# Another order for a planned kernel: nudged priorities, small halves last, recalibrated plan costs

## The chip, the cores and the metric

The kernel runs on one core of a Trainium2 chip. The metric is the device time of one execution in microseconds; the median over several runs counts. Five engines work side by side, each through its own instructions in the order in which they were written: TensorE (PE in the profile; its weight loads are PEld), VectorE (DVE), ScalarE (ACT), GpSimd (POOL) and SyncE (SP), which here only issues DMAs.

## The reference

Three stages follow each other. A delta rule runs over 768 positions for 32 (batch, head) pairs with a 48 x 48 state; a gated MLP (384 to 2048 to 384) works on the resulting 3072 tokens; a mixture of eight experts (384 to 1024 to 384) follows, weighted by a Sinkhorn-normalised gate:

```python
for t in range(S):                          # attention, S = 768
    y[:, :, t] = einsum('bhd,bhde->bhe', q_t, state)
    v_old = einsum('bhde,bhd->bhe', state, k_t)      # k_t normalised
    state = state + beta_t * einsum('bhd,bhe->bhde', k_t, v_t - v_old)
h = x @ w_in; x = (h * sigmoid(h)) @ w_out           # first MLP
P = exp(x @ w_gate - max)
for _ in range(8):                          # Sinkhorn
    P /= P.sum(1) + 1e-9; P /= P.sum(0) + 1e-9; P *= N / E
for e in range(E):
    out += P[:, e:e+1] * (maximum(x @ w1[e], 0) @ w2[e])
```

All is in float32, with inputs laid out by the host in their memory order only.

## The kernel before

**Halves.** Every large product is done in three matmuls of a rounded type: an operand is split into a high half (rounded by ACT) and a low half (what is left, by DVE or POOL); high x high, high x low and low x high are added up in PSUM.

**Attention and first MLP, interleaved.** Attention goes in 12 steps s of 64 positions. For a pair j of steps, `tri(j)` inverts small triangular matrices on DVE, 31 times a product (L555) and a subtraction (L553), then a scaling (L568). ACT copies the result (L571), SP writes it to DRAM (`rd`, `td`) and reads it back transposed (`rt`, `td`; L595, L603). Then each step is a chain of narrow matmul groups on PE with copies by ACT and DVE between: `z` (L614), `r` (L627), `c` (L646), `d` (L665), `y` (L680), the state's update `s` (L696, added by DVE in L701) and the transpose `t` (L713). The next step starts from that state. `gkq` (L405, L406) are the grams of keys and queries of later steps, whose loads `ke` go through SP.

Two steps make a batch b of 512 tokens for the first MLP, six batches in all. Each has 16 groups f: `moe_h` (PE, `h`, nine 128x512 matmuls, L740), the sigmoid on ACT (L746), the product on DVE (`sg`, L750), the high half on ACT (L754), the low half on POOL (`g`, L758), and `moe_o` (PE, `x2p`, nine matmuls, L782). The weights of this MLP are split in the kernel too, in 20 pieces, most of two groups f: `weight` loads one (`wr`, L869), ACT takes its absolute value and its high half (L873, L891) and DVE does seven instructions (L894, L895, L897, L899, L901, L903 and L905, which writes the low half in `w`). They are used six times; the first batch is where they must come in time.

**Experts.** Then the Sinkhorn normalisation (small PE groups `sk`, DVE and POOL) and 64 rounds of the expert stage. A round has 15 products `p` (L1213, three 128x512 matmuls each), whose results DVE, ACT and POOL add up and split, and 12 outputs `o` (L1300, six 128x384 matmuls each).

**What sets the order.** Nobody writes the order by hand: class `Order` is a list scheduler. Each group of work is added with its engine, a planned cost, its dependences and a priority (`add`). `emit` steps through a model of the run: for each engine it collects what could start (`ready`), takes among those within NEAR of the earliest the one with the highest priority (on PE, one of the same `turn` as the two before it is put back by ALT), advances the engine by the planned cost, and writes the instructions in that order. The plan's times are nothing but numbers in that model; on the chip an instruction waits for what it really needs. Until the first `moe_h`, `emit` also fills PE's planned gaps with matmuls on constant data (`idle`).

## Time and profile before

| | |
|---|---|
| runs of the kernel before (3) | 2260.31 us median, 2255.88 to 2264.96 |
| the profiled execution | 2263.14 us, span 2261.4 us |
| mean granted TensorE clock | 0.974 |
| busy PE / PEld | 2184.4 us (97%) / 1928.4 us (85%) |
| busy DVE / ACT / POOL | 1760.9 us (78%) / 1023.8 us (45%) / 1547.7 us (68%) |
| the chain that ended last, by engine | PE 64%, POOL 13%, DVE 10%, DMA 5%, issue 4%, ACT 2% |

The span is counted from the first to the last instruction; the rows below count their times from its start. The profile cuts the span into stretches with the busy time of each engine, so a stage can be read by itself: PE is idle for 77 us of the whole, and the granted clock says how much of the rest ran at the lower of the two levels (0.5 is 1.2 GHz, 1.0 is 2.4 GHz). Idle time on an engine that is not the last to be waited for costs nothing.

### The profile page before, as it was taken

The numbers are of one execution on the slowest core, as the hardware profiler recorded it, in microseconds if no ns is written. First come the engines' busy times: TensorE is split into PE (matmuls) and PEld (weight loads), VectorE is DVE, ScalarE is ACT, GpSimd is POOL, SyncE is SP. The second block draws the span as 40 slices with busy tenths as digits, with TensorE's granted clock in tenths as the row PEclk, the third lists the DMA queues.
The fourth block names the chain that finished last, engine by engine and source line by source line (L and its number), as shares of the span: only waits on it lengthen the run. The fifth ranks groups of instructions, "written<-read, shape, count | busy, mean of one in ns | idle before, by whom it ended". The sixth has DMA issues, their size and how long they took to land.

```text
span 2261.4 us, 40411 instructions
## 1 busy us (share of the span) xinstructions
PE 2184.4 (97%) x15750; PEld 1928.4 (85%) x15750; DVE 1760.9 (78%) x2999; ACT 1023.8 (45%) x1766; POOL 1547.7 (68%) x1387
## 2 busy tenths in 40 slices
PE   8988799999999899999999999989999999999999
PEld 8877578788877778889998999979999999999998
DVE  7695857464725698888888888897888888888887
ACT  2443333334344445454444545455454444445453
POOL 0223344445337688888788888877888888888884
PEclk9887999998989899999999999999999999999999
DMA  9767132314140201101111111111101111111101
GB/s 266 186 201 167 56 72 66 81 52 95 40 108 11 84 29 31 40 29 36 35 36 36 33 38 29 43 47 39 42 29 36 36 36 36 36 36 30 42 29 50
DMA packets 127424, 136.79 MB, mean 60 GB/s; under 512 B 83392, under 2 KB 91328, under 8 KB 127232
## 3 DMA queue, kind: packets, MB, share of 16 engines
q1 hardware_dynamic: 124864, 133.55, 21.4%
q8 instruction: 124, 2.03, 0.4%
q10 hardware_dynamic: 2368, 0.66, 0.2%
q14 instruction: 68, 0.56, 0.1%
HBM read 108.47 MB, written 25.69 MB: 59 GB/s over the span
## 4 chain that ended last, share of the span: by engine, by line
PE 64%; POOL 13%; DVE 10%; DMA 5%; issue 4%; ACT 2%; SPq 1%; DVEq 0%; POOLq 0%; ACTq 0%
PE o L1300 25%; PE p L1213 20%; PE x2p L782 6%; PE h L740 5%; DVE s L1022 4%; POOL room L1022 3%; POOL wa L1022 3%; POOL wraw L1022 2%; POOL h L1022 2%; DMA ke<-in_kq 2%; PE d L665 1%; POOL wb L1022 1%; DMA nd<-ke 1%; DVE acc L1316 1%; PE y L680 1%
## 5 line engine op out<-in xcount | busy, mean ns | idle before, releaser
L1213 PE MATMUL p<-room,wa 128*128 128x512 f32 x2880 | 732.8, 395 | 2.6 <-DVE s L1022 2.6
L1213 PEld LDWEIGHTS p<-room,wa 128*128 128x128 f32 x2880 | 537.2, 189 | 95.6 <-issue 3.0
L1300 PE MATMUL o<-wb,room 128*128 128x384 f32 x2784 | 601.2, 337 | 10.6 <-POOL room L1022 3.0
L1022 DVE TENSOR_TENSOR s<-s,p 128x512 f32<-128x512 f32 x704 | 475.8, 683 | 167.8 <-ACT s L1227 85.1
L1300 PEld LDWEIGHTS o<-wb,room 128*128 128x128 f32 x2784 | 496.7, 188 | 34.8 <-DVE acc L1316 9.3
L1022 POOL TENSOR_TENSOR room<-s,room 128x512 fp32r<-128x512 f32 x232 | 321.0, 1384 | 222.0 <-ACT s L1246 117.0
L1316 DVE SCALAR_TENSOR_TENSOR acc<-o,pr,acc 128x384 f32<-128x384 f32 x708 | 415.7, 610 | 15.0 <-PE o L1300 12.6
L1300 PE MATMUL o<-wb,h 128*128 128x384 f32 x1824 | 416.5, 336 | 6.1 <-DVE acc L1316 3.7
L1300 PEld LDWEIGHTS o<-wb,h 128*128 128x128 f32 x1824 | 327.7, 188 | 27.7 <-DVE acc L1316 2.8
L1022 POOL TENSOR_TENSOR wa<-wraw,wa 128x640 fp32r<-128x640 f32 x189 | 322.4, 1718 | 2.5 <-ACT wa L1116 2.5
L1244 ACT ACTIVATE room<-s 128x512 fp32r<-128x512 f32 x232 | 145.7, 628 | 382.5 <-DVE s L1022 382.3
L1022 POOL TENSOR_TENSOR wraw<-wraw 128x256 f32<-128x256 f32 x378 | 275.0, 748 | 20.5 <-issue 10.7
L758 POOL TENSOR_TENSOR g<-sg,g 128x512 fp32r<-128x512 f32 x96 | 129.8, 1353 | 219.9 <-ACT g L754 206.0
L1246 ACT ACTIVATE s<-s 128x512 f32<-128x512 f32 x384 | 243.1, 633 | 12.2
L782 PE MATMUL x2p<-g,w 128*128 128x512 f32 x864 | 228.9, 412 | 15.5 <-DVE w L905 5.8
L1116 ACT ACTIVATE wa<-wraw 128x640 fp32r<-128x640 f32 x189 | 138.2, 731 | 224.4 <-POOL wraw L1022 213.6
L1022 DVE TENSOR_TENSOR s<-p,s 128x512 f32<-128x512 f32 x320 | 219.5, 686 | 16.7 <-PE p L1213 2.0
L740 PE MATMUL h<-x,w 128*128 128x512 f32 x864 | 216.9, 398 | 5.9 <-DVE w L905 4.1
L782 PEld LDWEIGHTS x2p<-g,w 128*128 128x128 f32 x864 | 165.1, 196 | 59.3 <-POOL g L758 10.7
L1022 POOL TENSOR_TENSOR h<-s,h 128x512 fp32r<-128x512 f32 x152 | 208.7, 1373 | 7.9 <-ACT s L1246 7.8
L1022 DVE TENSOR_TENSOR s<-s,s 128x512 f32<-128x512 f32 x192 | 207.3, 1080 | 2.5
L740 PEld LDWEIGHTS h<-x,w 128*128 128x128 f32 x864 | 161.6, 190 | 44.2 <-DVE w L905 5.9
(177 smaller groups left out, 2260.9 us busy)
## 6 DMA issues: line engine op xcount, KB each, us to landing
wraw<-in_w SPq DMA_DIRECT2D x126, 384.0 KB, 3.0
kv<-in_kv SPq DMA_DIRECT2D x12, 768.0 KB, 5.8
ke<-in_kq SPq DMA_DIRECT2D x40, 192.0 KB, 4.4
kqp<-in_kq SPq DMA_DIRECT2D x40, 192.0 KB, 4.0
nd<-ke SPq DMA_DIRECT2D x20, 256.0 KB, 4.1
gd<-ke SPq DMA_DIRECT2D x20, 256.0 KB, 2.8
kqp<-gd SPq DMA_DIRECT2D x40, 128.0 KB, 3.8
wr<-in_w_in SPq DMA_DIRECT2D x6, 768.0 KB, 5.8
```

The lines of the kernel that those rows point to most:

```text
L665: nc.tensor.matmul(out=ps[o:o + 64, h], lhsT=rt[o:o + 64, bp, h], rhs=w[o:o + 64, h], start=True, stop=True)
L680: nc.tensor.matmul(out=ps[0:64, h], lhsT=t(slice(0, 112), 1)[:, h], rhs=x[0:112, 0, h], start=True, stop=True)
L740: nc.tensor.matmul(out=ps.rearrange("p (s t) -> p s t", s=2), lhsT=w[:, k, wl], rhs=X1[:, at, k, xl], start=n == 0, stop=n == 8)
L758: nc.gpsimd.tensor_tensor(out=g[:, 1], in0=T["sg", b, f], in1=f32(g)[:, 0], op=ALU.subtract)
L782: nc.tensor.matmul(out=T["x2p", b][j], lhsT=w[:, wl, 128 * j:128 * j + 128], rhs=g[:, gl], start=f == 0 and n == 0, stop=f == NF - 1 and n ...
L1022: e.tensor_tensor(out=out, in0=in0, in1=in1, op=o)
L1116: nc.scalar.activation(P2[key][:, :, 0], R(3 + 5 * g, 8 + 5 * g), AF.Copy)
L1213: nc.tensor.matmul(out=ps, lhsT=w[:, i, wl], rhs=x[:, xl], start=k == 0, stop=k == 2)
L1244: nc.scalar.activation(P2[key][:, 0], buf(x), AF.Relu)
L1246: op2("ACT", 0.52, lambda: nc.scalar.activation(buf(x), buf(x), AF.Relu), writes=[("s", n, x)], prio=PR_H)
L1300: nc.tensor.matmul(out=ps, lhsT=h[:, hl, 128 * i:128 * i + 128], rhs=w[:, wl], start=c == 0, stop=c == 5)
L1316: op2("DVE", 0.53, lambda A=A, pk=pk, t=t: nc.vector.scalar_tensor_tensor(out=A(), in0=P2[pk], scalar=P2["pr"][:, t, e:e + 1], in1=A(), op ...
```

## The change

Nothing is computed otherwise, and every engine has as many instructions as before, but for the `idle` matmuls: 347 instead of 283. What changes is the order.

- A table NUDGE of some 120 entries adds a number to the priority of a kind of operation (its engine, the function that issues it, its old priority). ALT and the NEAR windows get other values.
- Planned costs, the landing times of DMAs, latencies between instructions of one engine and the numbers of the plan's model of TensorE's clock are replaced by others. DVE additions with two inputs in SBUF and POOL's sums and low halves are now planned as excluding each other (`port`).
- In the plan alone, the reader of a split operand may start before its low half is done: by 1.2 us for `moe_o` (LATE), 0.45 (activations) or 0.85 (weights) for `moe_h` (SOON), 0.59 for the outputs (REST). The instructions still wait for the data.
- To go with that, the nine matmuls of a group are written with the half as the outer loop: those that read the second operand's low half, or the weights', come last.
- Where two engines' candidates start at the same planned time, the one that is ready earlier goes first.

```diff
-ALT = 9.5
+ALT = 12.4
-NEAR_DVE = 0.29
+LATE, SOON, REST = -1.2, -0.45, -0.59
+NEAR_DVE = 0.0
+NUDGE = {
+    ('DVE', 'weight', 1.5): -5.0, ('DVE', 'tri', 4): -3.8, ('PE', 'merge.z', 10): -4.9,
...
     def add(self, engine, cost, fn, ...
+        prio += NUDGE.get((engine, name, round(prio, 2)), 0.0)
...
-                if best is None or t < best[0]:
-                    best = (t, i, e)
+                if best is None or (t, r) < best[:2]:
+                    best = (t, r, i, e)
...
-            for k in range(KD):
-                for wl, xl in ((0, 0), (0, 1), (1, 0)):
+            for wl, xl in ((0, 0), (0, 1), (1, 0)):
+                for k in range(KD):
...
-        O["g", b, f] = [h, l]
+        O["g", b, f] = [h, (l, LATE)]
...
-            for j in range(KD):
-                for n, (wl, gl) in enumerate(((0, 0), (1, 0), (0, 1))):
+            for n, (wl, gl) in enumerate(((0, 0), (1, 0), (0, 1))):
+                for j in range(KD):
```

On DVE, before, the last turns of the first triangular inverse (`tri(0)`: `tmpu` and `tu` are its product and its result) stood alone:

```order
L555 TENSOR_TENSOR tmpu_97<-nu_95,tu_96 128x87
L553 TENSOR_TENSOR tu_96<-tu_96,tmpu_97 128x3x29
L555 TENSOR_TENSOR tmpu_97<-nu_95,tu_96 128x60
L553 TENSOR_TENSOR tu_96<-tu_96,tmpu_97 128x2x30
L555 TENSOR_TENSOR tmpu_97<-nu_95,tu_96 128x31
L553 TENSOR_TENSOR tu_96<-tu_96,tmpu_97 128x31
L568 TENSOR_TENSOR tu_96<-tu_96,du_100 128x1024
```

Now weight pieces (`w4`, `wt8`, `wt10`, `wr2`) stand between them; the changed kernel's L605, L607 and L620 are the L553, L555 and L568 of before, its L945 to L956 the weights' L894 to L905:

```order
L607 TENSOR_TENSOR tmpu_97<-nu_95,tu_96 128x87
L956 SCALAR_TENSOR_TENSOR w4_699<-wr1_525 128x2x384
L605 TENSOR_TENSOR tu_96<-tu_96,tmpu_97 128x3x29
L945 TENSOR_SCALAR wt8_771<-wt8_771 128x768
L607 TENSOR_TENSOR tmpu_97<-nu_95,tu_96 128x60
L946 TENSOR_SCALAR wt8_771<-wt8_771 128x768
L605 TENSOR_TENSOR tu_96<-tu_96,tmpu_97 128x2x30
L948 SCALAR_TENSOR_TENSOR wt8_771<-wr2_639,wt8_771 128x768
L607 TENSOR_TENSOR tmpu_97<-nu_95,tu_96 128x31
L945 TENSOR_SCALAR wt10_804<-wt10_804 128x768
L605 TENSOR_TENSOR tu_96<-tu_96,tmpu_97 128x31
L620 TENSOR_TENSOR tu_96<-tu_96,du_100 128x1024
```

In all, 19 weight instructions moved into the tail of this inverse: two pieces whole and five instructions of the next.

On DVE, in the first batch, the conversion of piece `wt20` (weights of groups 8 and up) stood behind the state updates of step 3 (`xs0_91<-xs0_91,s3_0`) and the masked keys of later steps (`kqp`):

```order
L447 TENSOR_TENSOR kqp1_86<-kqp1_86,mask_101 64x512 x2
L555 TENSOR_TENSOR tmpu_97<-nu_95,tu_96 128x31
L510 TENSOR_REDUCE ne4_2938<-sq4_0_2939 128x8
L701 TENSOR_TENSOR xs0_91<-xs0_91,s3_0_2941 48x384 x2
L510 TENSOR_REDUCE ne4_2938<-sq4_1_2961 128x8
L447 TENSOR_TENSOR kqp2_87<-kqp2_87,mask_101 64x512 x2
L894 TENSOR_SCALAR wt20_2343<-wt20_2343 128x768
L895 TENSOR_SCALAR wt20_2343<-wt20_2343 128x768
```

Now `w20` is complete within the second triangular inverse, ahead of the product `sg0_6` of the first batch:

```order
L605 TENSOR_TENSOR tu_96<-tu_96,tmpu_97 128x20x12
L950 TENSOR_SCALAR wr5_1882<-wr5_1882 128x768
L607 TENSOR_TENSOR tmpu_97<-nu_95,tu_96 128x247
L952 SCALAR_TENSOR_TENSOR wr5_1882<-wr5_1882 128x768
L605 TENSOR_TENSOR tu_96<-tu_96,tmpu_97 128x19x13
L954 TENSOR_SCALAR wr5_1882<-wt22_2062 128x768
L956 SCALAR_TENSOR_TENSOR w20_2228<-wr5_1882 128x2x384
L801 TENSOR_TENSOR sg0_6_2395<-h0_6_2361,sg0_6_2395 128x512
```

All 20 pieces now stand ahead of the last product of the first batch (`sg0_15`). Between `sg0_0` and the end of the second triangular inverse, DVE has 55 weight instructions, 62 of the inverse and 10 products (25, 52 and 6 before).

On PE, before, the first group of step 2 (`z2`) stood ahead of `h0_8`:

```order
L614 MATMUL z2_2453<-rt_93,td11_94 32x32 x32
L740 MATMUL h0_8_2490<-x1_106,w16_2424 128x512 x9
L627 MATMUL r2_2515<-zt2_2501,td11_94 32x32 x32
L740 MATMUL h0_9_2555<-x1_106,w16_2424 128x512 x9
L665 MATMUL d2_0_2577<-wq2_0_1712,rt_93 64x48 x16
L665 MATMUL d2_1_2602<-wq2_1_1752,rt_93 64x48 x16
```

Now it stands behind the `x2p` group of f = 11 (here the last three of its matmuls), so that 12 of the batch's 16 groups lie ahead of it:

```order
L833 MATMUL x2p0_0_1973<-g0_11_2835,w20_2228 128x512
L833 MATMUL x2p0_1_1974<-g0_11_2835,w20_2228 128x512
L833 MATMUL x2p0_2_1975<-g0_11_2835,w20_2228 128x512
L665 MATMUL z2_2890<-rt_93,td11_94 32x32 x32
L833 MATMUL x2p0_0_1973<-g0_12_2879,w24_2483 128x512
L833 MATMUL x2p0_1_1974<-g0_12_2879,w24_2483 128x512
L833 MATMUL x2p0_2_1975<-g0_12_2879,w24_2483 128x512
```

Between the last `x2p` of a batch and the first `h` of the next, some 17 narrow groups followed each other at the ends of the fourth and the fifth batch; now about 7 and 4 do. The Sinkhorn groups `sk` start later and stand further apart. In the rounds of the expert stage behind them, PE's order of products and outputs is the same.

## Rows read from the trace of the kernel before

**Rows 1.** Stretches of the span: length, then busy time of each engine.
```profile
core 0: us, PE busy (x) PEld busy (x) DVE busy (x) ACT busy (x) POOL busy (x), PEclk, DMA share, GB/s
0.00:106.00 106.00, 95.04 (x1799) 89.78 (x1799) 71.66 (x229) 37.74 (x68) 17.99 (x27) 0.89 0.88 231
106.00:263.00 157.00, 134.54 (x1860) 109.80 (x1856) 125.39 (x243) 67.12 (x111) 47.74 (x42) 0.87 0.57 151
263.00:743.00 480.00, 461.69 (x4568) 377.90 (x4567) 262.14 (x485) 177.63 (x322) 234.93 (x222) 0.96 0.27 64
743.00:860.00 117.00, 106.54 (x505) 91.80 (x504) 98.22 (x180) 61.09 (x110) 91.99 (x93) 0.94 0.17 58
860.00:1500.00 640.00, 636.99 (x3223) 576.60 (x3221) 553.56 (x860) 313.05 (x534) 541.96 (x472) 1.00 0.11 34
```

**Rows 2.** Timeline of PE, batches 0 and 1: start, length, engine, line.
```profile
106.12 1.21 PE L740 MATMUL h<-x,w 128*128 128x512 f32 x4
262.46 1.43 PE L740 MATMUL h<-x,w 128*128 128x512 f32 x5
```

**Rows 3.** Timeline of PE in the middle of a later batch.
```profile
586.83 2.20 PE L740 MATMUL h<-x,w 128*128 128x512 f32 x9
588.87 2.20 PE L782 MATMUL x2p<-g,w 128*128 128x512 f32 x9
```

**Rows 4.** What PE waited for, 106 to 263 us: total, times, longest.
```profile
PE gkq L405 <- DMA ke<-in_kq: 9.0, 4, 4.4
PE x2p L782 <- DVE w L905: 4.4, 2, 3.1
PE h L740 <- DVE w L905: 4.1, 3, 1.7
```

**Rows 5.** Timeline of DVE: end of the first inverse, then step 3 and `wt20`.
```profile
48.43 1.23 DVE L568 TENSOR_TENSOR tu<-tu,du 128x1024 f32<-128x1024 f32 x1
...
207.22 1.12 DVE L701 TENSOR_TENSOR xs<-xs,s 48x384 f32<-48x384 f32 x2 [2.04 <-PE s L697]
...
212.57 1.09 DVE L894 TENSOR_SCALAR wt<-wt 128x768 f32<-128x768 f32 x1
```

**Rows 6.** The chain that ended last, from 55 to 60 us, and at 175 us.
```profile
55.23 3.62 DMA ke<-in_kq
58.88 1.12 SPq L576
...
174.92 1.13 PE z L614 x64
```

**Rows 7.** Groups by line, DVE, 106 to 263 us: busy, mean ns, idle.
```profile
L553 DVE TENSOR_TENSOR tu<-tu,tmpu 128x112 f32<-128x112 f32 (+15 forms) x43 | 17.5, 408 | 0.9
...
L897 DVE SCALAR_TENSOR_TENSOR wt<-wr,wt 128x768 int32<-128x768 int32 (+1 forms) x15 | 12.6, 840 | 0.2
...
L899 DVE TENSOR_SCALAR wr<-wr 128x768 int32<-128x768 int32 (+1 forms) x15 | 8.0, 532 | 0.0
```

**Rows 8.** Timeline of ACT: the copy behind the second inverse.
```profile
158.52 2.09 ACT L571 ACTIVATE nu<-tu 128x1024 f32<-128x1024 f32 x1
```

**Rows 9.** Three shorter stretches; columns as in rows 1.
```profile
554.00:568.00 14.00, 14.00 (x186) 13.27 (x185) 5.90 (x15) 4.32 (x11) 9.04 (x11) 0.51 0.34 112
656.00:667.00 11.00, 11.00 (x168) 10.74 (x163) 2.94 (x7) 4.14 (x10) 2.09 (x3) 0.53 0.12 39
200.00:300.00 100.00, 82.00 (x710) 65.39 (x709) 81.16 (x174) 35.92 (x65) 31.29 (x30) 0.88 0.28 78
```

**Rows 10.** What PE waited for, 263 to 743 us; columns as in rows 4.
```profile
PE x2p L782 <- POOL g L758: 5.1, 6, 1.3
```

**Rows 11.** Timeline of POOL and DVE around 228 us.
```profile
228.32 1.46 POOL L758 TENSOR_TENSOR g<-sg,g 128x512 fp32r<-128x512 f32 x1 [0.80 <-ACT g L754]
228.54 1.64 DVE L897 SCALAR_TENSOR_TENSOR wt<-wr,wt 128x384 int32<-128x384 int32 x1
...
233.03 0.56 DVE L897 SCALAR_TENSOR_TENSOR wt<-wr,wt 128x384 int32<-128x384 int32 x1
```

More of the change, by code (lines that the diff above doesn't have):

```diff
@@ L60 @@
     QUEUES = ("SP",)
+    OWN = {"PE": 0.0, "DVE": 0.12, "ACT": 0.12, "POOL": 0.11, "SP": 0.08}
     LAT = {"PE": 0.2, "ACT": 0.16, "DVE": 0.14, "POOL": 0.1, "SP": 0.08}
@@ L67, in __init__, with add @@
         self.pools, self.slot = {k: [()] * n for k, n in pools.items()}, {}
-    TICK, PHASE, FULL = 10.24 / 3, 2.63, 2000
-    def add(self, engine, cost, fn, deps=(), prio=1.5, take=(), turn=None, cols=768, port=False):
+    TICK, PHASE, FULL, KEEP = 10.24 / 3, 2.53, 1000, 120
+    def add(self, engine, cost, fn, deps=(), prio=1.5, take=(), turn=None, cols=0, port=False, lands=None):
+        name = fn.__qualname__.replace("kernel.<locals>.", "").replace(".<locals>", "").replace(".<lambda>", "")
+        prio += NUDGE.get((engine, name, round(prio, 2)), 0.0)
         d = [x if isinstance(x, tuple) else (x, None) for x in deps]
-        self.ops.append((engine, cost, fn, d, prio, take, turn, cols, port))
+        self.ops.append((engine, cost, fn, d, prio, take, turn, cols, port, lands))
         return len(self.ops) - 1
@@ L99, in ready @@
             if lat is None:
-                lat = 0.0 if own == engine and engine not in self.QUEUES else self.LAT[own]
+                lat = self.LAT["SP"] if self.ops[d][9] else (self.OWN if own == engine else self.LAT)[own]
             at = max(at, end[d] + lat)
@@ L150, in emit @@
                         lane = lanes[-8] + 0.1 if e in self.QUEUES and len(lanes) >= 8 else 0.0
-                        c.append((max(r, now[e], lane, port["POOL" if e == "DVE" else "DVE"] if self.ops[i][8] else 0.0), i))
+                        r = max(r, now[e])
+                        c.append((max(r, lane, port["POOL" if e == "DVE" else "DVE"] if self.ops[i][8] else 0.0), i, r))
                 if not c:
@@ L185, in emit @@
                         order.append((now[e], len(order), None))
-                        now[e] = self.pe(now[e], 0.107, 256)
+                        now[e] = self.pe(now[e], 0.107, 80)
                     t = max(t, now[e])
-                    narrow = turn == 1 and cols != 150
+                    narrow = cols in (520, 221, 240, 390, 480, 530)
                     if narrow != tiled:
@@ L632, in merge @@
         sc.free(a, "a", [e1, e2])
-        c = O["r1", s] = op("PE", 1.13, r, [e1, e2] + O["tdl", s], prio=7.5 + FIRST[s], take=["a"], turn=1 if s else None, cols=512)
+        c = O["r1", s] = op("PE", 1.13, r, [e1, e2] + O["tdl", s], prio=7.5 + FIRST[s], take=["a"], turn=1 if s else None, cols=221)
         sc.free(a, "sg", [c])
@@ L785, in moe_o @@
         a = O["o", b, f] = op("PE", 2.045, pe, O["g", b, f] + O["wout", f] + prev, prio=4.5,
-                              take=["x"] if f == 0 else [], turn=0, cols=4608)
+                              take=["x"] if f == 0 else [], turn=0, cols=1430)
         sc.free(O["g", b, f][0], "g", [a])
@@ L996, with op2 @@
     last, lastw, readers, touched = NSTEP - 1, {}, {}, {}
-    def op2(engine, cost, fn, reads=(), writes=(), deps=(), **kw):
+    def op2(engine, cost, fn, reads=(), writes=(), deps=(), late=(), **kw):
         own = {"DVE": 0.13, "ACT": 0.14, "POOL": 0.1}
@@ L1003, in op2 @@
             x = lastw[k]
-            d.append((x, own.get(engine)) if sc.ops[x][0] == engine else x)
+            d.append((x, own.get(engine)) if sc.ops[x][0] == engine else (x, REST) if k in late else x)
         for k in writes:
@@ L1234, in add @@
             i = op2("DVE", 0.6, lambda: tt("DVE", buf(x), get(a), get(b), o), reads=[key(y) for y in (a, b) if y != x],
-                    writes=[("s", n, x)], take=["s"] if new else [], prio=PR_A)
+                    writes=[("s", n, x)], take=["s"] if new else [], prio=PR_A,
+                    port=PORT and isinstance(a, str) and isinstance(b, str))
             if new:
@@ L1302, in outputs @@
                 a = P2["pe"] = op2("PE", 1.042, pe, reads=[("h", n, f, j) for f in range(2)] + [("wb", wn(n), f) for f in range(2)], writes=[pk],
-                        deps=[(P2["pe"], 0.0)], take=["m"], turn=3, cols=2304, prio=PR_O)
+                        deps=[(P2["pe"], 0.0)], late=[("h", n, f, j) for f in range(2)], take=["m"], turn=3, cols=716, prio=PR_O)
                 if first and m == 0:
```

153 lines of the change are left out of this document (91 added, 62 removed), and 14 rows, old and new, of the table NUDGE.

## Prediction, made before the changed kernel ran

> **What bounds the kernel now.** I first read the busy time by stretches, cut where the stages change [rows 1]. From 860 us on, PE is busy 636.99 of 640 us at a granted clock of 1.00: the reader is to see an engine with nothing to give there but its own work. The other stretches are different. Ahead of the first `h` (0 to 106 us) no wide work exists. In the first batch (106 to 263, the starts of `h0_0` and `h1_0` [rows 2]) PE is busy 134.54 of 157 us at clock 0.87. In the batches behind it the idle time is 480 - 461.69 = 18.3 us at 0.96, around the Sinkhorn stage 117 - 106.54 = 10.5 us at 0.94. So about 11 + 22.5 + 18.3 + 10.5 = 62 us of PE's idle time, and nearly all its time at the lower clock, lie before 860 us.
>
> Second, a later batch in its steady state: `h` at 586.83 and `x2p` at 588.87, 2.04 us a group [rows 3]. Two groups alternate at that pace and nothing waits. The floor of the first batch is then, with 32 such groups, 65 us and the narrow groups. From rows 1: a mean clock of 0.87 means that 26% of 157 us = 41 us went by at 1.2 GHz; work done there would take half as long at 2.4 GHz, so at least 134.54 - 20 = 114 us stay.
>
> Third, why the first batch takes 157 us: the waits [rows 4] name the grams' loads (9.0 us) and the weights' low halves (4.4 + 4.1). The second lot is an order of DVE: step 3's state update stands at 207.22 (with a wait for PE before it), and piece `wt20` begins only at 212.57 [rows 5], so PE waits behind it for the weights of groups 8 and up. DVE had time, and stood behind narrow PE work.
>
> **The change, part by part.** The sum is made on the profiled execution, 2263.1 us, of which 2261.4 are the span; the median shown is 2.8 us lower.
>
> (1) *Start, +9.* 19 weight instructions now lie in the tail of the first inverse. Seven kinds take from 840 (L897) to 532 ns (L899) [rows 7], in the middle 0.69, so 13.0 us later ends L568, which ended at 49.66 [rows 5]. On the chain, the second write of `rd` (L576) went out at 58.88 behind a load that landed at 58.85 [rows 6], not behind the inverse: with the copy's 2.09 [rows 8] it could have gone at 51.8. Up to 7 us of the 13 are therefore cover, if the loads keep their place; but SP now also issues two more weight loads and two key loads ahead of it, and PE has five more gram groups to do before `h0_0`. Bounds 0 (the weights would otherwise have been done later, but still ahead of `h0_0`, and cost DVE there) and +13; I take +9, nearer to the inverse's price, since the rest of that chain is serial.
>
> (2) *First batch, 157 to 135: -22.* All pieces stand ahead of `sg0_15`, so the 8.5 us of waits for weights [rows 4] go, and the loads `ke`, of which two more go early, wait less. What is late next is the second inverse: step 2 needs it. Count DVE from `sg0_0` to its end: before 25 weight instructions, 52 of the inverse, 6 products; at 0.69, 0.41 (408 ns, L553 [rows 7]) and 0.69, as the products are of the same width, 42.7 us. In the trace the copy behind it starts 158.52 - 106.12 = 52.4 us after the first `h` [rows 2, 8], so 9.7 us are start-up and waits. Now 55, 62 and 10 make 70.3; with the same 9.7 the copy starts at +80. From the copy to `z2` it was 174.92 - 158.52 = 16.4 us [rows 6, 8]: +96. From `z2` to the end of step 3's update 208.34 - 174.92 = 33.4 [rows 5, 6]: +130. Transposes and halves up to `h1_0`: my estimate is 5, some ten dependent instructions of half a microsecond, the size of the short ones in rows 7. Sum 135, above PE's floor of 114. Bounds: -43 (PE's floor) and 0 (below).
>
> (3) *Batches 1 to 5: -16.* At the ends of batches 3 and 4, PE was busy in every microsecond of 554 to 568 and 656 to 667 and yet at 0.51 and 0.53 [rows 9], the 1.2 GHz level: 25 us of narrow groups only, that would take half at the other level. With 7 and 4 narrow groups in a row instead of 17, I take 10 of those 12.5 us. Low halves written last in a group let its first six matmuls begin earlier: the 5.1 us of waits of `x2p` for `g` [rows 10], taken as gone, and 1 more of the other waits. Bounds +5 (spread narrow groups interrupt wide ones more often) and -28 (all of the 18.3 idle and 10).
>
> (4) *Sinkhorn: -4*, of 10.5 us idle and a clock of 0.94 [rows 1]; the small groups stand apart, so that products lie between them. Bounds -12 and +5, as the rounds behind could wait for the gate's result.
>
> (5) *Expert rounds: 0.* The order is the same and PE has 3 us of 640 to give; ±4.
>
> Halves last, in a group that finds both halves ready, costs nothing: the same nine matmuls with the same loads of weights, 2.04 us. For `h` they go into one bank as before. For `x2p` neighbours now write three banks in turn; the row of 2.20 for nine [rows 3] was taken with one bank after the other, and I exclude no loss: 0.02 us a group would be 2 us in 96 groups.
>
> +9 - 22 - 16 - 4 = -33: 2230 on the profiled execution, 2227 beside the median.
>
> A rule of the Trainium skill speaks against term (3). In rows 9 the clock is at 1.2 GHz while PE never waits. The skill ("TensorE: Matmul & The Clock Gate", section "HAM oscillation — how this bites in real kernels") puts such falls down to waits between bursts; by it, shortening runs without a gap would give nothing back (a rival, below). The rows differ from the rule, and the sum goes by them.
>
> **Rivals.**
>
> *Narrow runs were not what lowered the clock (4%).* Then shorter ones leave the clock at the ends of batches 3 and 4 where it was, the 10 us of term (3) stay out, and the time is 2237. For it: the clock is low in the first batch too (0.87 [rows 1]), where PE does wait. Against: rows 9 have no idle time at all.
>
> *The gain is given back (14%).* Each batch is paced by its steps, and the third inverse, which batch 2 needs, stands where it stood in DVE's work. Then the first batch's 22 us come back as waits of `z4` for `rt`, and +9 - 16 - 4 = -11 is left: 2249. For it: the steps are one chain through all batches. Against: in 263 to 743 DVE is busy 262 of 480 us [rows 1], so the inverses have room.
>
> *POOL and DVE exclude each other (7%).* At 228.54 a weight instruction took 1.64 us while POOL's low half ran from 228.32 for 1.46; the same form took 0.56 at 233.03 [rows 11]: 1.1 us lost. DVE now has 10 instead of 6 groups' low halves beside the dense weights before the second inverse ends; if each stops it for 1.1 us, z2 is 10 x 1.1 = 11 us later and the time 2238. The skill says that this pair of engines takes turns for a whole instruction ("SBUF — State Buffer", section "SBUF: two separate sides"); the pair of rows agrees. Against a general stop: from 200 to 300 us DVE and POOL are busy 81.16 and 31.29 of 100 us together [rows 9], so at least 12 us ran side by side.
>
> *The plan moves, the waits stay (11%).* LATE, SOON and REST change no wait on the chip. If the rest is reshuffling, what is left is the halves: 5.1 and 8.5 us of waits at best [rows 4, 10], less the +9 at the start: 2255 to 2260.
>
> *Slower (12%): the second inverse becomes the limit.* It shares DVE with 30 more weight instructions, and `z2` now stands behind 12 of 16 groups, so four groups (16 us of `h` and `x2p` [rows 3]) are all that PE has to lay beside the 33 us of steps 2 and 3. If DVE's waits grow with its work (52.4 / 42.7 = 1.23), the copy starts at +86 and `z2` at +103; narrow groups alone at 1.2 GHz, as in rows 9, stretch 33.4 to some 50, as the clock was partly lower already: `h1_0` at +158, no gain, while the start costs its 13. With nothing won behind it: 2263 + 13 + 1 = 2277, or 2274 beside the median. It decides from a copy at +84 us after the first `h` on. Against it: weights are spread between dependent instructions of the inverse, where DVE had nothing else.
>
> **How the numbers follow.** The forecast, 52% (2205 to 2246); the others as given. About 0.5%, 11 us, is what a measurement of this kernel can tell from no change: faster is below 2249, slower above 2272. Faster: 52, 4 and 7, and half of the 14, 70%; same: the other 7, the plan-only case and a little of the slower one, 19%; slower 11%. The range: down to 2202 (the first batch near PE's floor and term (3) near its bound, half each), up to 2262, which takes in the two rivals at 2249 to 2260.
>
> **What would show it.** `h0_0` at 115 (0 to 13 later than 106). `h1_0` about 250 instead of 262.5, the copy behind the second inverse at +80 of `h0_0`, no wait for L905's successor above a microsecond in the first batch. No stretch of over 10 us at 0.5 at the ends of batches 3 and 4. The first `p` at about 714 instead of 743, a group at 2.04 in the batches, and the rounds' time as before. I am wrong in (2) if `h1_0` stays behind 258, in (3) if the time from `h1_0` to the first `p` stays at 481, in (5) if the rounds' time changes by more than 4 us.

## The result, and the profile after

The changed kernel takes 2181.33 us (median of 4 runs, 2172.4 to 2184.06) beside 2258.1 for the kernel before (4 runs): a ratio of 0.9649, interval 0.9612 to 0.9687. Faster was forecast, at 2227 within 2202 to 2262; the gain is 77 us where 31 were forecast, and the time lies below the range. The profiled execution took 2183.1 us, span 2181.3, so it stands for the median.

Cut at the first matmul of each stage (first `h` of a batch, first `p` of a round), the spans divide so, in us; the last column is what the prediction's sum has:

| stage | before | after | difference | forecast |
|---|---|---|---|---|
| start, to `h0_0` | 106.1 | 121.8 | +15.7 | +9 |
| batch 0, to `h1_0` | 156.3 | 115.8 | -40.5 | -22 |
| batches 1 to 5, to the first `p` | 481.0 | 449.8 | -31.2 | -16 |
| rounds 0 to 3 (with Sinkhorn) | 104.3 | 93.7 | -10.6 | -4 |
| rounds 4 to the end | 1413.6 | 1400.2 | -13.4 | 0 |

The stretches of the changed kernel's span at these cuts; columns as in [rows 1], stretches in order: start, batches 0, 1, 3, rounds 0 to 3, rounds 4 to 31:

```profile
0.00:121.80 121.80, 106.23 (x1927) 101.50 (x1927) 88.28 (x250) 46.31 (x78) 16.62 (x24) 0.85 0.83 221
121.80:237.60 115.80, 114.95 (x1756) 95.29 (x1753) 98.38 (x210) 59.69 (x105) 48.52 (x45) 1.00 0.66 181
237.60:329.50 91.90, 91.19 (x1083) 75.06 (x1082) 59.28 (x119) 35.56 (x65) 51.17 (x50) 1.00 0.37 82
...
426.20:520.70 94.50, 92.71 (x1049) 75.36 (x1050) 59.02 (x114) 34.94 (x65) 49.45 (x48) 0.98 0.35 74
...
687.40:781.10 93.70, 89.53 (x438) 78.56 (x437) 82.67 (x160) 50.27 (x93) 79.79 (x80) 0.96 0.19 68
781.10:1425.20 644.10, 644.10 (x3279) 588.52 (x3278) 559.82 (x879) 323.02 (x551) 545.62 (x484) 1.00 0.11 34
```

Batch 0 is the line to read first. PE was busy 134.54 of 157 us at 0.87 [rows 1]; now 114.95 of 115.8 at 1.00. Some 22 us of idle time are gone, and some 20 us of busy time, as much as the clock of 0.87 had cost by the prediction's reckoning. What PE still waits for in this batch, in two lines (total, times, longest), against three of 4 to 9 us before [rows 4]:

```profile
PE gkq L457 <- DMA ke<-in_kq: 0.5, 1, 0.5
PE h L791 <- DVE sg L801: 0.3, 1, 0.3
```

The chain that ended last, by engine, is now mostly PE's work (before: PE 64%, POOL 13%, DVE 10%):

```profile
PE 82%; DVE 6%; DMA 5%; POOL 3%; ACT 1%; SPq 1%; issue 1%; DVEq 0%; POOLq 0%; ACTq 0%
```

### The profile page after: what moved, and what is told of

It reads as the page before. It is cut to its first block, busy times and chain, and to the rows that moved or that the text cites. A ratio compares the mean times of both kernels' runs of the same rounds, so it can differ in the third digit from the quotient of the medians.

```text
span 2181.3 us, 40538 instructions
## 1 busy us (share of the span) xinstructions
PE 2148.3 (98%) x15814; PEld 1912.0 (88%) x15814; DVE 1741.8 (80%) x2999; ACT 1021.5 (47%) x1766; POOL 1539.6 (71%) x1387
## 4 chain that ended last, share of the span: by engine, by line
PE 82%; DVE 6%; DMA 5%; POOL 3%; ACT 1%; SPq 1%; issue 1%; DVEq 0%; POOLq 0%; ACTq 0%
PE o L1352 36%; PE p L1264 29%; PE x2p L833 5%; PE h L791 4%; PE d L716 1%; DVE s L1073 1%; DMA kqp<-gd 1%; PE gkq L456 1%; DMA ke<-in_kq 1%; DVE tmpu L607 1%; PE idle L1454 1%; PE y L731 1%; POOL g L809 1%; DVE tu L605 1%; DVE sg L801 1%
## 5 line engine op out<-in xcount | busy, mean ns | idle before, releaser
L1352 PE MATMUL o<-wb,room 128*128 128x384 f32 x2784 | 792.2, 337 | 3.9 <-POOL room L1073 2.4
L1352 PE MATMUL o<-wb,h 128*128 128x384 f32 x1824 | 609.5, 336 | 0.2 <-ACT room L1212 0.2
L1352 PEld LDWEIGHTS o<-wb,room 128*128 128x128 f32 x2784 | 512.3, 188 | 26.2 <-POOL room L1073 3.0
L1368 DVE SCALAR_TENSOR_TENSOR acc<-o,pr,acc 128x384 f32<-128x384 f32 x708 | 429.1, 614 | 83.2 <-PE o L1352 82.9
L1073 POOL TENSOR_TENSOR room<-s,room 128x512 fp32r<-128x512 f32 x232 | 305.6, 1320 | 152.9 <-ACT s L1298 146.7
L1352 PEld LDWEIGHTS o<-wb,h 128*128 128x128 f32 x1824 | 342.8, 188 | 14.1 <-ACT s L1298 0.6
L1073 POOL TENSOR_TENSOR wraw<-wraw 128x256 f32<-128x256 f32 x378 | 284.5, 761 | 11.2 <-DMA wraw<-in_w 1.9
L833 PE MATMUL x2p<-g,w 128*128 128x512 f32 x864 | 219.2, 402 | 4.2 <-ACT g L805 2.6
L791 PE MATMUL h<-x,w 128*128 128x512 f32 x864 | 211.0, 395 | 0.6 <-DVE sg L801 0.6
L1073 DVE TENSOR_TENSOR s<-s,s 128x512 f32<-128x512 f32 x192 | 173.2, 902 | 2.8
```

Of the source, the lines that this page charges most:

```text
L791: nc.tensor.matmul(out=ps.rearrange("p (s t) -> p s t", s=2), lhsT=w[:, k, wl], rhs=X1[:, at, k, xl], start=n == 0, stop=n == 8)
L833: nc.tensor.matmul(out=T["x2p", b][j], lhsT=w[:, wl, 128 * j:128 * j + 128], rhs=g[:, gl], start=f == 0 and n == 0, stop=f == NF - 1 and n ...
L1073: e.tensor_tensor(out=out, in0=in0, in1=in1, op=o)
L1352: nc.tensor.matmul(out=ps, lhsT=h[:, hl, 128 * i:128 * i + 128], rhs=w[:, wl], start=c == 0, stop=c == 5)
L1368: op2("DVE", 0.53, lambda A=A, pk=pk, t=t: nc.vector.scalar_tensor_tensor(out=A(), in0=P2[pk], scalar=P2["pr"][:, t, e:e + 1], in1=A(), op ...
```

## The experiments

All numbers by stage come from one profiled execution each, cut as above; median and ratio come from timed runs beside the kernel before. Batch 0 and the rounds decide most of what follows. Two executions of one order differ: after and after_again by 5.4 us in batch 0, before and halves_only (the same order of groups) by 6.2 us in the start and 4.5 us in the later rounds. Differences by stage of less than some 6 us are therefore not read as effects.

| kernel | start | batch 0 | batches 1-5 | rounds 0-3 | rounds 4- | median | ratio to before (95%) |
|---|---|---|---|---|---|---|---|
| before | 106.1 | 156.3 | 481.0 | 104.3 | 1413.6 | 2258.1 | |
| after | 121.8 | 115.8 | 449.8 | 93.7 | 1400.2 | 2181.3 | 0.965 (0.961-0.969) |
| halves_only | 112.3 | 154.0 | 474.8 | 103.4 | 1409.1 | 2255.3 | 1.000 (0.998-1.001) |
| halves_undone | 113.1 | 117.5 | 459.7 | 91.8 | 1400.5 | 2186.1 | 0.970 (0.967-0.973) |
| lead_undone | 119.3 | 120.0 | 447.6 | 99.8 | 1399.9 | 2189.5 | 0.968 (0.963-0.973) |
| table_undone | 120.6 | 133.4 | 458.2 | 94.7 | 1403.7 | 2208.6 | 0.979 (0.976-0.981) |
| table_alt_near_undone | 106.4 | 149.3 | 464.4 | 101.4 | 1411.1 | 2232.0 | 0.989 (0.988-0.991) |
| weights_after_inverse | 105.3 | 137.1 | 463.0 | 98.4 | 1399.5 | 2209.0 | 0.977 (0.973-0.982) |
| w20_after_step3 | 118.1 | 156.6 | 463.7 | 91.6 | 1400.3 | 2239.1 | 0.990 (0.985-0.994) |
| near_dve_undone | 104.5 | 243.7 | 464.8 | 101.0 | 1409.4 | 2328.9 | 1.030 (1.026-1.035) |
| near_dve_zero_only | 116.7 | 119.9 | 475.6 | 104.8 | 1449.3 | 2273.8 | 1.005 (1.002-1.007) |
| port_undone | 122.8 | 115.1 | 445.9 | 100.1 | 1413.8 | 2199.2 | 0.972 (0.967-0.978) |
| port_only | 105.9 | 154.0 | 476.1 | 104.4 | 1469.2 | 2313.5 | 1.023 (1.019-1.026) |
| near_dve_and_port_only | 118.4 | 120.8 | 486.1 | 103.7 | 1571.2 | 2394.3 | 1.058 (1.054-1.063) |
| port_and_tie_only | 106.4 | 161.5 | 468.3 | 99.5 | 1407.4 | 2243.3 | 0.992 (0.989-0.995) |
| near_port_tie_only | 120.0 | 119.5 | 475.4 | 96.5 | 1404.1 | 2222.0 | 0.983 (0.980-0.986) |
| tie_undone | 120.9 | 127.4 | 449.5 | 97.8 | 1403.4 | 2199.1 | 0.972 (0.969-0.974) |
| more_idle | 128.9 | 115.0 | 453.1 | 91.7 | 1399.8 | 2191.8 | 0.969 (0.967-0.970) |
| idle_014 | 120.9 | 119.4 | 449.2 | 93.6 | 1400.9 | 2182.0 | 0.966 (0.963-0.968) |
| after_again | 120.4 | 121.2 | 446.4 | 91.7 | 1400.2 | 2176.7 | 0.963 (0.961-0.965) |

A caution that holds for all but halves_only, halves_undone, idle_014 and after_again: an edit of the plan's inputs makes `emit` plan everything anew, so a stage that the edit does not name moves by some us too.

**The halves.** In the kernel before, and back in the changed one:

```diff
-            for k in range(KD):
-                for wl, xl in ((0, 0), (0, 1), (1, 0)):
+            for wl, xl in ((0, 0), (0, 1), (1, 0)):
+                for k in range(KD):
```

halves_only. 

> The kernel before with one part of the change: the three loops that write the small halves last, with every group in its old place. Theory (the order of the groups carries the gain): at most the waits for low halves go, 5 us for g and 8.5 us for the weights, so 2245 to 2258 us where the kernel before has 2258. Rival (the halves carry it, since a wide group may start before its low operand is there): 2200 to 2230, with the first batch (h0_0 to h1_0, 156 us before) under 140.

halves_undone. 

> The changed kernel with only the three loops put back (high and low halves alternate), every group in its new place. Theory: 2185 to 2197; the plan now starts a group up to 1.2 us ahead of its low half, so some of the 96 x2p groups pay up to 1.2 us. Rival (the halves carry the gain): 2220 or more.

Alone the halves are worth nothing (1.000, to 0.2%). Undone in the changed kernel they cost 4.7 us of median, with intervals that overlap; by stage, 10 us in batches 1 to 5, where the plan starts `x2p` ahead of its low half. So they are worth little, and only in the new order. That the leads are the reason is likely but not shown: no run leaves out both.

**The leads.** `LATE, SOON, REST = None, None, None`, and the weights' -0.85 likewise.

> The changed kernel planned with LATE, SOON and REST at their ordinary latencies: the plan waits for low halves, halves still written last. Theory (the leads move little): 2181 to 2192, first batch within 3 us. Rival (threes of h and x2p groups and the leads make the later batches shorter): h1_0 to the first p 465 or more instead of 450, 2196 or more.

8 us of median, with intervals that overlap; batches 1 to 5 are not longer at all (447.6), and what its profile is longer by stands in rounds 0 to 3 (99.8). The theory that they move little held for the whole. Batch 0 is 4 us longer where 3 were allowed, but after_again has 121.2 there too.

**The table, and the windows.** First `NUDGE = {}`, then also `ALT = 9.5` and the four NEAR as before.

table_undone. 

> The changed kernel with the table of 120 priorities empty; recalibrated costs, leads, ALT, NEAR and the halves stay. DVE still has the weight pieces early in this order (33 weight instructions ahead of the end of the first inverse, w20 ahead of step 3's update). Theory (early weights are the largest part): first batch 116 to 125 us, 2190 to 2205. Rival (the searched priorities are the gain): 2235 or more.

table_alt_near_undone. 

> The changed kernel with the table empty and ALT and the NEAR windows as before, so that the recalibrated costs, the leads and the halves are left. DVE's order is then like that of before at the two places (14 weight instructions ahead of the first inverse's end, 23 between sg0_0 and the second inverse's end, the rest behind). Theory: the start is back at 106, the first batch at 140 or more, 2215 to 2245. Rival (the recalibrated model is the gain, wherever the weights stand): 2195 or less.

Without the table 27 us are lost; in the profile, 18 in batch 0 and 11 in batch 1 (the weights are early, but not all: 14 weight instructions stand behind `sg0_15`). With the windows put back as well, the weights are late and batch 0 takes 149.3 us: both as the theory of the early weights has it, the first past its upper numbers (125 and 2205).

**Where the weights stand on DVE.** Three kernels from the changed one, and one from the kernel before. In the first two the plan alone gets an added dependence for the first instruction of a weight piece n:

```diff
+    for n in range(4, 2 * NF):      # weights_after_inverse
+        if ("wfirst", n) in O: sc.ops[O["wfirst", n]][3].append((O["td2", 0], None))
+    for n in range(20, 2 * NF):     # w20_after_step3
+        if ("wfirst", n) in O: sc.ops[O["wfirst", n]][3].append((O["sa", 3, 0], None))
-NEAR_DVE = 0.0                      # near_dve_undone
+NEAR_DVE = 0.29
-NEAR_DVE = 0.29                     # near_dve_zero_only, in the kernel before
+NEAR_DVE = 0.0
```

weights_after_inverse. 

> The changed kernel, planned anew with the conversion of weight pieces from w4 on not before the end of the first triangular inverse (14 weight instructions ahead of it, as before the change, not 33). Theory of the start (each weight instruction in the inverse's tail delays the first h by its own length, 15 us in all): h0_0 at 106 to 109; if the first batch is held by PE's floor it stays at 116 to 120 and the whole is 2168 to 2174. Rival (the weights then come late for the first batch): the batch grows by the 13 us that the start gains, 2181 or more.

w20_after_step3. 

> The changed kernel, planned anew with the conversion of pieces from w20 on not before step 3's first state update, as it stood before the change. Theory (this place is what starved PE in the first batch): PE waits for w again, first batch 135 to 150 us, 2203 to 2215. Rival (the batch was shortened by something else: narrow groups, loads of ke, halves): first batch under 122, 2181 to 2188.

near_dve_undone. 

> The changed kernel planned with NEAR_DVE = 0.29 as before. The weights then stand later than even in the kernel before (none between sg0_0 and the second inverse's end, w20 behind step 3's update). Theory: the start gains 8 to 15 us, the first batch takes 155 to 190, 2225 to 2260. Rival (the table alone keeps PE fed): 2200 or less.

near_dve_zero_only. 

> The kernel before with one number changed: NEAR_DVE = 0.0 for 0.29. In its plan a weight instruction then takes the 0.13 us gaps between dependent instructions of the triangular inverses: 33 weight instructions ahead of the first inverse's end instead of 14, w20 ahead of step 3's update; 14 weight instructions still stand behind sg0_15 (none in the changed kernel). Theory (early weights on DVE are the largest single cause, about 50 of the 77 us): 2205 to 2225, first batch 120 to 135 us. Rival (they need the other numbers to pay, or their start price eats them): 2240 or more.

With `wt20` behind step 3, batch 0 takes 156.6 us again, more than was expected, and the clock is at 0.86 again, as in [rows 1]. Batch 1 takes 103.2 instead of 91.9, and the whole 2239.1: this one place gives back 58 of the 77 us. Its stretch (columns as in rows 1), and the longest of PE's waits there:

```profile
118.10:274.70 156.60, 128.37 (x1853) 103.79 (x1850) 117.91 (x260) 60.25 (x101) 52.72 (x48) 0.86 0.58 150
```

```profile
PE h L791 <- ACT w L942: 12.0, 2, 10.9
PE x2p L833 <- DVE w L956: 3.1, 2, 1.8
```

The wait for ACT's high half is one for DVE: ACT copies what DVE has prepared (`wt`, L948). When the window alone is put back, pieces come so late that PE stands still three times for some 31 us, and the batch and the whole lie far above what was expected:

```profile
PE h L791 <- DVE w L956: 61.3, 2, 31.0
PE x2p L833 <- DVE w L956: 32.5, 2, 30.7
```

And in the kernel before, the one number NEAR_DVE brings batch 0 from 156.3 to 119.9 us. So the place of the weights is needed, and moving them nearly empties batch 0 of waits. But the cut at `h1_0` flatters this run: the last pieces still stand behind `sg0_15`, two `x2p` groups of batch 0 still run behind `h1_0`, and batch 1 grows from 107.8 to 116.2 us:

```profile
236.60:352.80 116.20, 109.38 (x1199) 90.01 (x1199) 76.36 (x168) 40.12 (x77) 56.17 (x54) 0.94 0.33 78
```

With the start, 10.6 us longer, batch 2 begins 17.6 us earlier than before; in the changed kernel it begins 40.8 us earlier. The table sets beside each other how many weight instructions DVE still has behind the last product of batch 0, and the two batches:

| kernel | behind `sg0_15` | batch 0 | batch 1 |
|---|---|---|---|
| before | 11 | 156.3 | 107.8 |
| w20_after_step3 | 7 | 156.6 | 103.2 |
| weights_after_inverse | 13 | 137.1 | 108.1 |
| table_undone | 14 | 133.4 | 103.2 |
| near_dve_zero_only | 14 | 119.9 | 116.2 |
| near_port_tie_only | 7 | 119.5 | 111.2 |
| tie_undone | 0 | 127.4 | 93.5 |
| after | 0 | 115.8 | 91.9 |

In all twenty profiles, batch 1 takes 92 to 95 us where no weight instruction is left behind `sg0_15`, and 102 to 119 where some are. Why the number does it can be read in the code: dependent instructions of an inverse are planned 0.13 us apart, so with a window of 0 an independent weight instruction, which could start at once, is taken first; with 0.29 the inverse's next instruction lies within the window and goes by priority.

My theory of the start was half right. Without the 19 weight instructions the first `h` comes at 105.3, 16.5 us earlier (three gram groups and 40 constant matmuls are gone from the start as well, so not all of it need be theirs); but the pieces are then late, and batches 0 and 1 lose 21 and 16 us (137.1 and 108.1). The rival is right with more than it asked for: the weights in the first inverse are well paid.

near_dve_zero_only also showed a price that I had not seen: the rounds from 4 on take 36 us more, so that the whole is 0.5% slower than before, where 2205 to 2225 was expected. PE waits for the outputs' sums on DVE (L1316):

```profile
PE o L1300 <- DVE acc L1316: 32.7, 49, 1.2
```

**Turns of DVE and POOL in the rounds.** The flags `port=True` on the sums and low halves of the rounds, in the plan only; and the rule for equal planned times:

```diff
-PORT = True                                          # port_undone
+PORT = False
-  ... prio=PR_A)                                     # port_only, in the kernel before
+  ... prio=PR_A, port=isinstance(a, str) and isinstance(b, str))
-                if best is None or t < best[0]:      # port_and_tie_only
+                if best is None or (t, r) < best[:2]:
```

port_undone. 

> The changed kernel planned with PORT = False: DVE's sums of two tiles in SBUF and POOL's weight sums and low halves may overlap in the plan of the expert stage, as before the change. Theory (the expert stage's 13 us come from DVE and POOL taking turns by plan: the sum of two tiles of sums took 902 instead of 1080 ns): the sum is back at about 1080 ns, the stage from the first p 10 to 15 us longer, 2190 to 2196. Rival (that gain is from the halves or from chance): within 4 us of 2181.

port_only. 

> The kernel before, with the plan's exclusion (port) put on DVE's sums of two tiles and POOL's weight sums and low halves of the expert stage, and nothing else. Theory (taking turns by plan gives the expert stage its 13 us): the sum of two tiles at about 900 ns instead of 1080, the time from the first p 10 to 20 us shorter, 2238 to 2248. Rival (it needs the new costs as well): 2255 to 2260.

near_dve_and_port_only. 

> The kernel before with both of these: NEAR_DVE = 0.0 and the port flags of the expert stage. Theory (two separate causes in two stages): the gains add up, 2190 to 2212; it is then within 30 us of the changed kernel without its table, leads, costs and halves. Rival (they meet the same bound): no more than the better one of the two alone.

port_and_tie_only. 

> The kernel before with the port flags of the expert stage (which alone made it 56 us longer there) and the rule that of two engines' candidates at the same planned time the one that was ready earlier goes first. Theory (with port, DVE and POOL come free at the same planned time, and without the rule the same engine always wins, so POOL's low halves are planned and run late): PE's 42.7 us of waits for POOL in the outputs go, and the stage from the first p is 10 to 20 us shorter than before, 2238 to 2250. Rival (other costs of the recalibration are the partner of port): still 2290 or more.

near_port_tie_only. 

> The kernel before with three things: NEAR_DVE = 0.0, the port flags and the rule for ties. Theory (early weights in the first batch, turns with the rule in the expert stage, and the rest of the change on top): first batch 116 to 125, expert stage at most 5 us longer than in the changed kernel, 2195 to 2215. Rival (as above): the expert stage is over 40 us longer than before.

tie_undone (the changed kernel with the first line of the rule). 

> The changed kernel planned without the rule for ties. Theory: PE waits for POOL or DVE in the expert stage, 30 to 100 us longer from the first p on, 2215 to 2280. Rival (the recalibrated costs or the table carry the expert stage): within 8 us of the changed kernel.

port_undone gives the whole gain of the later rounds back (1413.8, before 1413.6) and 6 us of the first: without turns in the plan, the rounds are as before. They are needed and not enough: table_alt_near_undone keeps them and the rule for ties, and has 1411.1 in the later rounds, no gain clear of noise. And port_only did the opposite of what I expected: 56 us longer, and with NEAR_DVE = 0 158 us. PE waits there for POOL's low halves, and in the second for DVE's sums. The longest wait of each of the two kernels, over the whole span, port_only first:

```profile
PE o L1301 <- POOL room L1022: 42.7, 54, 0.9
```

```profile
PE p L1213 <- DVE s L1022: 117.0, 29, 4.5
```

With the rule for ties the same flags win: 1407.4 and 1404.1, and 2222.0 us with all three, 7 above the range expected. Where both engines exclude each other, both candidates become possible at one planned time, the end of the other's instruction; without the rule the engine that happens to be looked at first takes it, again and again. That reading of the code fits the runs, which show the pair of them. It is not the only remedy: in the changed kernel without the rule the rounds lose 7 us in all, not 30 to 100, so the theory fell there. Neither did the rival's number come: the whole is 18 us longer, 12 of them in batch 0. Something else in the changed kernel (the recalibrated costs, the other windows or the table) must prevent it too; which stays open.

One more step of my reasoning fell. I had taken the duration of DVE's sum of two tiles as the measure. Its line in the changed kernel, in port_undone and in near_dve_and_port_only (count, busy, mean ns, idle):

```profile
L1073 DVE TENSOR_TENSOR s<-s,s 128x512 f32<-128x512 f32 x192 | 173.2, 902 | 2.8
```

```profile
L1073 DVE TENSOR_TENSOR s<-s,s 128x512 f32<-128x512 f32 x192 | 206.3, 1074 | 4.2
```

```profile
L1022 DVE TENSOR_TENSOR s<-s,s 128x512 f32<-128x512 f32 x192 | 161.8, 843 | 2.1
```

The slowest kernel of all has the shortest sum of these three. What decides is whether PE waits behind it, not how long it takes.

**Constant matmuls in the start.** Planned at another length, so that more or fewer fit the gaps (347 in the changed kernel):

```diff
-                        now[e] = self.pe(now[e], 0.107, 80)
+                        now[e] = self.pe(now[e], 0.08, 80)   # more_idle, 553 (and gaps from 0.2 us)
+                        now[e] = self.pe(now[e], 0.14, 80)   # idle_014, 267
```

more_idle. 

> The changed kernel with more matmuls on constant data in PE's planned gaps ahead of the first h (planned 0.08 us each and in gaps from 0.2 us). The same order gave the first h at 121.8 us with a granted clock of 0.76 in 80 to 106 us in one execution and at 113.1 with 1.00 in another. Theory (the clock makes this spread and the gaps make the clock): 0.95 or more in 80 to 106, h0_0 at 111 to 116, 2171 to 2178. Rival (the added matmuls only delay the narrow groups, or the clock falls by another cause): 2181 or more.

idle_014. 

> The changed kernel with 267 matmuls on constant data ahead of the first h instead of 347 (planned at 0.14 us each, every other order the same). With 553 of them the granted clock was 1.00 nearly throughout the start and yet the first h came at 128.9. Theory (they run on PE in the way of the narrow groups when they take longer than planned, so fewer are better): h0_0 at 108 to 118, 2170 to 2180 where the changed kernel beside it has 2181. Rival (fewer let the clock fall and the narrow groups get slower): h0_0 at 120 or more, no gain.

after_again. 

> The changed kernel itself, beside the one with fewer constant matmuls: 2176 to 2186; its first h anywhere from 113 to 123, as in the runs with the same order.

With more of them the clock is full up to 80 us and 0.93 behind it, and still `h0_0` comes at 128.9, 7 us later; the median is 10 us up, as the rival had it. Two stretches of more_idle, then one of the changed kernel:

```profile
60.00:80.00 20.00, 20.00 (x362) 19.43 (x361) 10.69 (x21) 5.02 (x6) 0.95 (x1) 1.00 0.66 187
80.00:106.00 26.00, 20.76 (x485) 18.69 (x486) 17.09 (x38) 12.62 (x25) 4.15 (x4) 0.93 0.93 180
```

```profile
80.00:106.00 26.00, 24.80 (x650) 23.16 (x648) 19.28 (x42) 14.66 (x29) 4.00 (x3) 0.76 0.77 183
```

PE is full from 60 to 80 us and DVE less busy than in the changed kernel (10.69 of 20 us, there 15.97). The chain that ended last has 131 constant matmuls in it, and behind them a gram, for which ACT waits 8.7 us before it can copy the first inverse's result (start, length):

```profile
55.79 14.87 PE idle L1454 x131
```

```profile
72.72 1.08 ACT L472 ACTIVATE ke<-gkq 128x512 f32<-128x512 f32 x2 [8.72 <-PE gkq L457]
```

So here the constant matmuls stand in the way. Fewer change nothing (0.966 and 0.963, intervals overlap; `h0_0` at 120.9), as the rival of idle_014 had it. So a fuller clock that is bought with more constant matmuls does not shorten the start, nor do fewer of them. No variant beats the changed kernel.

## Why the prediction was wrong

The direction was right, and so was the cause of the largest gain. Three steps failed: the sum of (2) put 18 us too much above PE's floor, (3) left out 15 us of the same cause in the next batch, and (4) and (5) put the rounds 20 us too low, because only PE's order was looked at. The start, 7 us dearer than forecast, hides a part of it.

(2) **Batch 0, -22 forecast, -40.5 measured: a mis-sized term.** The cause was named rightly: the place of `wt20`, as w20_after_step3 shows by itself. So was the floor, 114 us against 115.8 measured here and 121.2 in after_again. The failed step is the sum that set 135 above that floor. Its links in the trace of the changed kernel, the copy behind the second inverse and the issues of `rd` and `rt` behind it, and the chain's `z2` (start, length):

```profile
192.72 2.18 ACT L623 ACTIVATE nu<-tu 128x1024 f32<-128x1024 f32 x1 [0.34 <-DVE tu L620]
```

```profile
194.93 0.47 SPq L628 DMA_DIRECT2D rd<-nu  x1
...
197.94 2.35 SPq L647 DMA_DIRECT2D rt<-rd  x4
```

```profile
202.61 1.13 PE z L665 x64
```

The copy starts at +71 from the first `h` (121.82), not +80: the 55 weight instructions took 0.58 us each, not 0.69, and I counted instructions one behind the other that overlap (DVE's durations from `sg0_0` to the inverse's end add up to 73.2 us and cover 63.7). From the copy to `z2` it is 9.9 us, not 16.4 as in [rows 6, 8]: the transposed read goes out 5.2 us behind the copy's start; before, it was 8.5, with writes of `td` and two weight loads ahead of it on SP:

```profile
165.58 0.90 SPq L869 DMA_DIRECT2D wr<-in_w_in  x2
166.52 0.43 SPq L603 DMA_DIRECT2D td<-td  x1
167.05 4.46 SPq L595 DMA_DIRECT2D rt<-rd  x4
```

From `z2` to `h1_0` it is 35 us, against 39. PE was idle 0.9 us in the whole batch: the chain that I took for the next bound ran beside PE's work, so the floor decided, and the bound of -43 was the better value. In after_again, the same order, the copy starts at +76 and the batch is 5 us longer, so a part of the distance between 115.8 and 135 is luck of this execution.

(3) **Batches 1 to 5, -16 forecast, -31.2 measured.** Batches 3 and 4 gave 9.9 and 2.4 us (104.4 to 94.5 and 97.9 to 95.5), 12 together where 10 were taken for their ends. The low clock there is gone: 0.51 and 0.53 before [rows 9], 1.00 now in the last 20 us of either batch:

```profile
500.00:520.00 20.00, 20.00 (x399) 16.54 (x395) 14.34 (x26) 9.47 (x20) 12.56 (x14) 1.00 0.38 102
596.00:616.00 20.00, 19.89 (x367) 16.63 (x361) 7.14 (x14) 8.27 (x18) 5.09 (x6) 1.00 0.03 9
```

That it belonged to long runs of narrow groups agrees with this, but no run changed that alone. The half that I missed is batch 1: 107.8 to 91.9 us. Its stretch before, and batch 3's:

```profile
262.50:370.30 107.80, 101.72 (x1113) 81.33 (x1112) 65.62 (x137) 37.04 (x68) 48.13 (x48) 0.98 0.33 75
467.00:571.40 104.40, 102.88 (x1120) 86.67 (x1116) 57.83 (x112) 37.43 (x70) 51.23 (x51) 0.92 0.36 81
```

Before, the last `x2p` of batch 0 ran until 276 us, 14 us into batch 1. That is the tail of the same late weights: w20_after_step3, which moves pieces from `w20` on and nothing else by hand, has 103.2 us there, 11 of the 16 us, and the kernels of the table of batch 0 and batch 1 divide the same way (each planned anew, so that is agreement and not a test). Most of what (3) missed was therefore the cause of (2), and I priced it in one stage only.

(4) and (5) **The rounds, -4 forecast, -24 measured.** This is the largest miss. I looked at the order on PE, saw it unchanged, and put nothing on the later rounds. The order of DVE and POOL had changed, and port_undone shows that the later rounds' 13 us need the plan's turns between the two. Rounds 4 to 31 and rounds 32 and 33 before, then rounds 32 and 33 after:

```profile
847.80:1498.30 650.50, 647.49 (x3278) 586.48 (x3277) 560.97 (x872) 321.43 (x550) 552.20 (x483) 1.00 0.11 34
1498.30:1553.30 55.00, 47.49 (x235) 41.62 (x234) 45.37 (x64) 31.61 (x56) 38.80 (x30) 1.00 0.19 65
```

```profile
1425.20:1475.40 50.20, 48.11 (x236) 43.34 (x235) 42.16 (x63) 30.54 (x55) 38.69 (x30) 0.97 0.22 71
```

In rounds 4 to 31, PE was idle 3 us before (650.5 us long) and 0.0 now (644.1); what shortened the other 3 us, which count as busy, is not resolved. The larger loss of idle time lies behind them: 7.5 of 55.0 us before, 2.1 of 50.2 now. The rival of POOL and DVE was looked for in batch 0, where the copy came earlier than forecast and not later; it stood in the rounds, with the other sign.

The Trainium skill ("SBUF — State Buffer", section "SBUF: two separate sides") says that a VectorE instruction with two SBUF inputs and a GpSimd instruction that reads SBUF take turns. The trace of the kernel before agrees: of the 192 sums of two SBUF tiles, the 29 without a POOL instruction beside them took 683 ns, the others 1150 on average. Planning for it did not pay by itself: in the kernel before, the flags alone lengthened the sum to 1274 ns (port_only) and the rounds with it, and they won only with the rule for ties. In the changed kernel they win without that rule too (1403.4 in tie_undone).

(1) **Start, +9 forecast, +15.7 measured**, above the bound of +13. It is 113 to 123 us in other runs of the same order, and 106 to 112 with the order of before, so the size is known only as +1 to +17. I took cover for 4 of the 13 us. There was none on balance: the end of the inverse (L620) moved by 15.1 us, and the copy behind it stood on ACT behind two copies of grams (L472), which waited for PE:

```profile
63.50 1.22 DVE L620 TENSOR_TENSOR tu<-tu,du 128x1024 f32<-128x1024 f32 x1
```

```profile
67.84 1.09 ACT L472 ACTIVATE ke<-gkq 128x512 f32<-128x512 f32 x2 [4.51 <-PE gkq L457]
68.82 1.98 ACT L623 ACTIVATE nu<-tu 128x1024 f32<-128x1024 f32 x1
```

That made the copy 19 us later than before, and the rest of the chain was 3 us shorter. Of the five more gram groups that I had named and not priced, the trace shows three (19 ahead of `h0_0` against 16), and they are not shown to be the reason: table_undone has 17 and starts at 120.6 all the same. What the two copies wait for is a gram behind 95 constant matmuls on PE; in idle_014, with fewer of these, the same gram waited for its load `ke`, which landed at 65.3 us, and the copy came no earlier (69.13). On the chain, in the changed kernel and in idle_014:

```profile
53.33 12.46 PE idle L1454 x95
```

```profile
56.58 8.67 DMA ke<-in_kq
```

So the constant matmuls and the load (63.9 us in the changed kernel) end close together, and fewer of the one gained nothing; no run took away both. How the spread of 10 us between executions of one order arises stays open: the clock in 80 to 106 us differs (0.76 here, 1.00 in halves_undone at 113.1), but more_idle had 0.93 and was late.

Of the rivals, *the gain is given back* is refuted (batch 1 gained too), *the plan moves, the waits stay* as well (the waits went, and halves_only by itself has 2255.3), and *the second inverse becomes the limit* too: the copy was at +71 where it decided from +84 on. *Narrow runs were not what lowered the clock* did not come as stated: the clock at those two ends rose. The signs named for the forecast came, most of them further than named: `h1_0` at 237.6 (250 expected), the copy at +71 (+80), no wait for L956 in batch 0, no low clock at the ends of batches 3 and 4, first `p` at 687 (714); the sign against (5), rounds changed by more than 4 us, came as well.

## What to carry to other kernels

Where a stage is starved and its engine's own work is known, take that work for a candidate of equal weight: here it was the time once the cause was removed. A longer chain put above it must be shown link by link, with waits of the old order left out, and the leftovers that the stage pushed into the next one belong to its price. An order that is unchanged on the busiest engine says nothing of the engines that feed it; compare those too. Do not judge a stage by its own cut alone: near_dve_zero_only shortened batch 0 by 36 us and gave 8 of them back in the next. And a planner's parts are not additive: flags that are worth 18 us in the changed kernel cost 50 in the kernel before, and one window that wins 36 us in one stage loses as much in another.

## What the runs showed of the hardware

In batch 0, PE was idle 22 us and the granted clock was 0.87; without the waits the clock was 1.00 and PE's busy time 20 us less, so this stage gave back nearly twice its idle time. At the ends of batches 3 and 4, PE worked on narrow groups without a pause, and the clock was 0.51 and 0.53 all the same [rows 9], the lower level. In the start, 553 constant matmuls instead of 347 kept the clock at 1.00 to 80 us, and the first wide group still came 7 us later.

On DVE, a 128x512 sum of two SBUF tiles took 683 ns in the kernel before where no POOL instruction ran beside it, and 1150 on average where one did. The same sum with one input in PSUM took 683 on average, beside POOL or not:

```profile
L1022 DVE TENSOR_TENSOR s<-s,p 128x512 f32<-128x512 f32 x704 | 475.8, 683 | 167.8 <-ACT s L1227 85.1 <-PE p L1213 36.0 <-ACT s L1246 12.2
```
